# One transfer instead of two for each kept weight and sum, a new order of all steps, and the last stores in the order of their tiles

## The chip, the cores and the metric

The kernel runs on one core of one Trainium2 chip. The metric is the device time in microseconds of one execution. A core has a matrix engine (PE), a vector engine (DVE), a scalar engine (ACT), a general engine (POOL) and a queue engine that only issues transfers (SP). Each of them works through its own instructions strictly in order and waits for the others by semaphores. POOL issues transfers too.

## The reference

What is computed is linear attention, followed by a normalized and gated two-layer network. The shapes are 8 batches, 8 heads, 576 positions and 64 dimensions, so 4608 tokens of 512 numbers, and an inner width of 1536.

```
q_s = exp(q - max(q, axis=-1));  q_s = q_s / (sum(q_s, axis=-1) + 1e-9)
k_s = exp(k - max(k, axis=2));   k_s = k_s / (sum(k_s, axis=2) + 1e-9)
kv  = einsum('bhsd,bhse->bhde', k_s, v)
x   = einsum('bhsd,bhde->bhse', q_s, kv) -> 4608 x 512
xn  = x / sqrt(mean(x * x, axis=-1) + 1e-6) * rms_g
g   = xn @ w_gate;  val = xn @ w_val
out = (g * 1/(1 + exp(-g)) * val) @ w_out
```

The three weights come as 64-bit floats and are turned into 32-bit ones on the chip.

## The kernel before

**Precision.** Each matrix product is made in three passes: an operand is split into a high part that PE takes as it is and a low part (the rest), and high times high, high times low and low times high are added up in PSUM. Names that end in `_hi` and `_lo` are the steps that make these parts (a cast, then a subtraction).

**Tiling.** The 4608 tokens are nine blocks of 512. Blocks 0 to 2 are computed directly, in units s = 0 to 35: twelve units to a block, one for each 128 columns of the inner width. A unit has f1.s.0 and f1.s.1 (gate and value, 12 matmuls each, into the two banks of `ps_gv`), g_mul.s and h_mul.s (DVE, L965 and L972, which read and free those banks), silu.s (ACT), h_hi.s and h_lo.s, and f2.s (12 matmuls into the four banks of `ps_o`). Blocks 3 to 8 are three pairs in a scheme of Winograd: seven products (pp) on sums of weights and sums of inputs, DVE steps that combine them (c_...), then gate, hm, the split hp_hi and hp_lo, the second layer f2p and the stores put.p.t.n. The attention of a block runs in between, in small steps: k_load, k_max, k_diag, k_sub, k_exp, k_mm (the product of k and v, L566 on PE), kv_hi, kv_lo, and likewise q_load, q_max and so on. They use the two banks of `ps_a`. k and v tiles have two buffers each, q tiles three.

**Weights.** In block 0 the weights are loaded and converted (load_w, conv_...); in block 1 (units 12 to 23) they are split again and the split weights are kept: w_keep (L901), o_keep (L905) and, for sums of weights of the Winograd scheme, s_add, s_hi, s_lo and s_keep (L946) write them to DRAM from SP's queue. In the end of block 2 w_back and o_back, and in the pairs w_in and o_in, read them back by transfers that POOL issues.

**What sets the order.** A table of 3101 steps, the string ORDER, is written out by hand. The program goes through it from the front and calls each step's function; a letter behind a colon picks the engine (A is ACT, D is DVE, P is POOL), and without one the function's own is taken. So the table sets the order of each engine's instructions. Buffers, semaphores and the waits that follow from them are put in by the framework: a tile in a pool with n buffers waits until the tile n places ahead is read, and a transfer on SP is tied to one of eight semaphores, so that it also waits for the transfer eight ahead of it to land.

**The last steps.** put copies a finished bank of PSUM to SBUF and stores it (L1206). Of the tiles of the last group of tokens, number 2 and 3 are copied to tiles named `gs` and the rest to tiles named `ot`, which have two buffers; number 3 is copied and stored in two halves, by ACT (L1200) and DVE (L1202).

A helper `copy` records copies of several steps under one line (L388), and `scaled` under L395, k_diag's among them.

Of the kernel before, what the change touches and what calls it, by code (L numbers as in the profile page):

```python
# [27 lines left out]
load_w.1.1 k_load.1.0 q_eps0.0.0 q_eps0.0.2 k_tr.0.2 warm.2.2 q_rec0.0.0 k_max0.0.3 warm.2.10 load_w.0.2 q_rec0.0.2
q_mul0.0.0:P k_tr.0.3 k_top.0.2 load_w.2.0 q_max0.0.3 k_diag.0.2:A load_w.2.1 k_rows.0.2 q_mul0.0.2:P q_sum0.0.1
q_t0.0.0 q_load0.1.0 k_top.0.3 k_sub.0.2 q_sub0.0.3:P k_diag.0.3:A warm.2.11 q_c0.0.0:A k_rows.0.3 warm.2.3 k_eps.0.0  # L30
k_exp.0.2 load_w.1.2 k_sub.0.3 q_t0.0.2 load_w.3.0 q_exp.0.3 load_w.3.1 k_max0.0.1 k_mm.0.2 k_exp.0.3 load_w.2.2
load_w.3.2 q_eps0.0.1 k_rec.0.0 q_c0.0.2:A q_rec0.0.1 k_load.1.1 k_tr.0.1 q_sum0.0.3 warm.2.13 q_mul0.0.1:P
kv_norm0.0.0:A k_mm.0.3 k_top.0.1 k_eps.0.2 k_diag.0.1:A q_eps0.0.3 k_rec.0.2 conv_mul.0.0 q_load0.1.1 q_rec0.0.3
k_rows.0.1 k_eps.0.3 q_mul0.0.3:P q_x0.0.0 k_sub.0.1 kv_norm0.0.2:A conv_low.0.0.1 q_t0.0.1 k_rec.0.3 conv_shift.0.0
k_exp.0.1 q_load0.1.2 conv_sign.0.0 q_x0.0.2 x_hi.0.0:A conv_add.0.0.1 q_c0.0.1:A x_lo.0.0 warm.2.12 x_sq.0.2 warm.2.5
x_sq.0.0 k_mm.0.1 x_hi.0.2:A q_t0.0.3 conv_mul.0.1 k_eps.0.1 x_lo.0.2 kv_norm0.0.3:A v_ones.1.0 conv_shift.0.1 n_sum0.0
v_load.1.0 q_c0.0.3:A k_rec.0.1 conv_sign.0.1 conv_low.0.1.1 warm.2.6 q_x0.0.3 k_max.1.0 kv_norm0.0.1:A conv_add.0.1.1
# [5 lines left out]
w_hi.1.0.2:A f1.0.0.2.1 f1.0.0.2.2 f1.0.0.2.3 f1.0.1.2.0 conv_low.3.0.2 conv_sign.0.2 w_lo.1.0:P f1.0.1.2.1 f1.0.1.2.2
f1.0.1.2.3 n_rows.0 k_tr.1.0 conv_low.2.2.1 conv_add.0.2.1 k_top.1.0 g_mul.0 k_diag.1.0:A k_rows.1.0 q_sum0.1.0 f1.1.0
silu.0 w_lo.1.1:P load_w.4.0 k_sub.1.0 load_w.4.1 load_w.4.2 n_cols.0 v_ones.1.1 v_load.1.1 conv_mul.2.0 q_eps0.1.0
h_mul.0 conv_mul.2.1 conv_shift.2.0 f1.1.1 k_exp.1.0 conv_shift.2.1 conv_sign.2.0 conv_sign.2.1 conv_mul.1.2 q_rec0.1.0
f2.0 conv_add.2.0.2 g_mul.1 conv_mul.3.0 conv_shift.1.2 conv_low.3.2.1 conv_shift.3.0 silu.1 conv_sign.1.2 q_mul0.1.0:P
conv_sign.3.0 w_hi.2.0.2:A h_mul.1 conv_add.1.2.1 k_mm.1.0 q_load0.1.3 k_max.1.1 conv_mul.3.1 warm.2.9 w_lo.2.0:P
f1.2.0 conv_low.4.0.2 k_eps.1.0 load_w.5.0 conv_shift.3.1 load_w.5.1 w_lo.2.1:P conv_low.4.2.1 k_rec.1.0 load_w.5.2
conv_sign.3.1 k_load.1.2 kv_norm0.1.0:A q_max0.1.1 conv_add.3.0.2 conv_mul.2.2 q_t0.1.0 g_mul.2 kv_hi.1.0:A f1.2.1  # L50
q_c0.1.0:A conv_shift.2.2 silu.2 q_max0.1.2 conv_mul.4.0 conv_sign.2.2 q_sub0.1.1:P w_hi.3.0.2:A conv_shift.4.0
conv_add.2.2.1 q_x0.1.0 q_max0.1.3 q_exp.1.1 conv_sign.4.0 f2.1 w_lo.3.1:P load_w.6.0 x_hi.1.0:D load_w.6.1 x_sq.1.0
load_w.6.2 h_mul.2 q_sub0.1.2:P conv_mul.4.1 x_lo.1.0 conv_low.5.0.2 q_sub0.1.3:P conv_shift.4.1 q_sum0.1.1
conv_mul.3.2 v_ones.1.2 kv_lo.1.0:P f1.3.1 v_load.1.2 conv_sign.4.1 conv_low.5.2.1 w_lo.3.0:D conv_mul.4.2
conv_shift.3.2 conv_add.4.0.2 q_exp.1.2 conv_shift.4.2 q_exp.1.3 f1.3.0 conv_sign.3.2 conv_low.6.0.2 conv_sign.4.2
conv_add.3.2.1 conv_mul.5.0 k_max.1.2 w_hi.4.0.2:A conv_add.4.2.1 load_w.7.0 f2.2 conv_shift.5.0 conv_mul.5.1
load_w.7.1 g_mul.3 load_w.7.2 conv_low.6.2.1 w_lo.4.0:P load_w.8.0 conv_shift.5.1 silu.3 load_w.8.1 conv_sign.5.0
load_w.8.2 w_lo.4.1:P conv_sign.5.1 conv_mul.5.2 q_sum0.1.2 conv_add.5.0.2 k_tr.1.1 f1.4.0 o_hi.4:A k_top.1.1 h_mul.3
k_diag.1.1:A conv_shift.5.2 q_sum0.1.3 conv_low.7.0.2 o_lo.4:P conv_sign.5.2 k_rows.1.1 f1.4.1 k_sub.1.1 w_hi.5.0.2:A
conv_add.5.2.1 g_mul.4 k_exp.1.1 q_eps0.1.1 w_lo.5.0:P load_w.10.0 q_rec0.1.1 load_w.10.1 f2.3 load_w.10.2 q_mul0.1.1:D  # L60
conv_mul.6.0 w_lo.5.1:P conv_mul.6.1 q_load.2.0 conv_shift.6.0 silu.4 conv_shift.6.1 conv_sign.6.0 conv_sign.6.1
k_mm.1.1 o_hi.5:A h_mul.4 conv_add.6.0.2 conv_mul.7.0 f1.5.0 k_eps.1.1 h_hi.4:A k_rec.1.1 k_load.1.3 conv_shift.7.0
kv_norm0.1.1:A conv_sign.7.0 conv_low.8.0.2 h_lo.4:P q_t0.1.1 g_mul.5 w_hi.6.0.2:A f1.5.1 q_c0.1.1:D o_lo.5:P
conv_mul.7.1 conv_mul.6.2 conv_shift.7.1 w_lo.6.0:P silu.5 conv_shift.6.2 conv_low.7.2.1 conv_sign.7.1 w_lo.6.1:P f2.4
conv_low.8.2.1 conv_sign.6.2 conv_mul.7.2 conv_add.7.0.2 h_mul.5 conv_low.10.0.2 conv_shift.7.2 k_max.1.3 h_hi.5:A
q_x0.1.1 conv_low.10.2.1 conv_add.6.2.1 f1.6.0 conv_sign.7.2 x_hi.1.1:A q_max.2.0 x_sq.1.1 h_lo.5:P x_lo.1.1
w_hi.7.0.2:A q_half.2.0 conv_mul.8.0 conv_add.7.2.1 f1.6.1 g_mul.6 conv_mul.8.1 conv_shift.8.0 silu.6 w_lo.7.0:P
load_w.9.0 conv_shift.8.1 o_hi.6:A load_w.9.1 load_w.9.2 kv_hi.1.1:A conv_sign.8.0 x_acc.1.1:P f2.5 conv_sign.8.1
conv_mul.8.2 w_lo.7.1:P h_mul.6 conv_shift.8.2 h_hi.6:A conv_add.8.0.2 conv_sign.8.2 conv_mul.9.0 f1.7.0 o_hi.7:A
conv_shift.9.0 conv_sign.9.0 conv_mul.9.1 o_lo.6:P w_hi.8.0.2:A conv_shift.9.1 k_tr.1.2 f1.7.1 h_lo.6:P g_mul.7  # L70
conv_low.9.0.2 k_top.1.2 conv_sign.9.1 w_lo.8.0:P k_diag.1.2:A silu.7 conv_mul.9.2 q_eps0.1.2 v_ones.1.3 q_eps0.1.3
k_rows.1.2 q_rec0.1.2 conv_add.9.0.2 v_load.1.3 f2.6 h_mul.7 conv_low.9.2.1 k_sub.1.2 h_hi.7:A conv_shift.9.2 k_exp.1.2
q_rec0.1.3 conv_sign.9.2 q_mul0.1.2:P f1.8.0 o_lo.7:P q_load.2.1 w_hi.9.0.2:A w_lo.8.1:P q_t0.1.2 g_mul.8 w_lo.9.0:P
k_mm.1.2 q_c0.1.2:A silu.8 f1.8.1 k_eps.1.2 conv_add.9.2.1 k_load.2.0 k_rec.1.2 kv_norm0.1.2:D h_lo.7:P conv_mul.10.0
conv_mul.10.1 q_max.2.1 w_lo.9.1:P f2.7 kv_hi.1.2:A conv_shift.10.0 conv_shift.10.1 conv_add.8.2.1 conv_sign.10.0
conv_sign.10.1 q_mul0.1.3:P conv_mul.10.2 load_w.11.0 f1.9.0 load_w.11.1 h_mul.8 o_hi.8:A load_w.11.2 conv_add.10.0.2
conv_shift.10.2 o_hi.9:A q_load.2.2 h_hi.8:A k_max.2.0 q_x0.1.2 g_mul.9 o_lo.8:P w_hi.10.0.2:A conv_sign.10.2 f1.9.1
# [248 lines left out]
def linear_attention_then_gated_ffn(ctx: ExitStack, tc, q, k, v, w_gate, w_val, w_out, rms_g, out):  # L326
    nc = tc.nc
# [569 lines left out]
    def w_keep(s):  # L897
        i, odd = divmod(s % NF, 2)
        at = A21 if odd else A11
        for m in range(2):  # L900
            nc.sync.dma_start(wd[i][m][:, at:at + 2], wh_[s][:, m].bitcast(F32))  # L901
# [347 lines left out]
```

## Time and profile before

| | |
|---|---|
| median of 3 runs | 981.62 us (979.29 to 983.41) |
| the profiled execution | 976.97 us, its span 975.2 us |
| PE busy | 944.7 us, 97% of the span |
| DVE, ACT, POOL busy | 681.7, 456.5 and 524.7 us |
| mean granted clock of PE | 0.99 |
| transferred | 202.32 MB, mean 207 GB/s |
| kept weights and sums: transfers issued on SP | 24 of 512 KB (L901), 24 and 48 of 256 KB (L905, L946) |

The profile is of one execution. Its span runs from the first to the last instruction, and the time is a little longer. In timelines, a row has the start, the duration, the engine, the line of the kernel, the operation, what it writes and reads, and in brackets how long the engine had been idle and what released it. SPq is the queue of SP. A wait is put down to the one that came last.

### The profile page before, as it was taken

What the parts mean: (1) busy time and instruction counts of PE and PEld (TensorE: products, weight loads), DVE (VectorE), ACT (ScalarE), POOL (GpSimd) and SP (SyncE); (2) the same over time, 40 slices, a digit from 0 to 9 for tenths busy, and PEclk for the clock granted to TensorE, in tenths of its full rate; (3) what the DMA queues carried; (4) which work ended last, traced back from release to release, by engine and by line L of the source; (5) the groups of instructions that cost most, each with busy time, mean ns of one, the idle gap of its engine ahead of it and who ended that gap; (6) DMA issues with size and microseconds to landing.
All of it is one profiled execution on the core that took longest, in us unless ns stands there. A gap on an engine that the chain in (4) does not pass through costs nothing.

```text
span 975.2 us, 14167 instructions
## 1 busy us (share of the span) xinstructions
PE 944.7 (97%) x4681; PEld 760.8 (78%) x4681; DVE 681.7 (70%) x1436; ACT 456.5 (47%) x721; POOL 524.7 (54%) x557
## 2 busy tenths in 40 slices
...
GB/s 240 236 299 205 115 46 265 272 293 302 259 218 214 206 224 178 190 243 218 258 211 182 144 239 150 193 261 151 215 173 258 217 160 233 214 191 195 89 203 140
DMA packets 166836, 202.32 MB, mean 207 GB/s; under 512 B 105924, under 2 KB 127724, under 8 KB 162156
## 3 DMA queue, kind: packets, MB, share of 16 engines
...
HBM read 160.49 MB, written 40.89 MB: 207 GB/s over the span
## 4 chain that ended last, share of the span: by engine, by line
PE 75%; DMA 8%; DVE 7%; SPq 5%; issue 3%; ACT 1%; POOL 1%; DVEq 0%; ACTq 0%; POOLq 0%
PE ps_gv L1101 17%; PE ps_o L1101 12%; PE ps_gv L960 10%; PE ps_o L1188 10%; PE ps_a L1101 7%; PE ps_o L997 6%; PE ps_a L1188 5%; PE ps_gv L1188 5%; DMA qt<-in_q_dram 3%; SPq L634 2%; DMA kt<-in_k_dram 2%; PE ps_a L566 1%; DMA raw<-in_moe_w_val_dram 1%; SPq L946 1%; PE ps_a L772 1%
## 5 line engine op out<-in xcount | busy, mean ns | idle before, releaser
L960 PE MATMUL ps_gv<-xh,w 128*128 128x512 f32 x576 | 193.2, 402 | 0.2 <-DVE gs L972 0.2
L1101 PE MATMUL ps_gv<-x,ring 128*128 128x512 f32 x576 | 142.2, 392 | 0.0
L960 PEld LDWEIGHTS ps_gv<-xh,w 128*128 128x128 f32 x576 | 108.9, 189 | 26.0 <-issue 1.3
L1101 PEld LDWEIGHTS ps_gv<-x,ring 128*128 128x128 f32 x576 | 107.2, 188 | 22.5
L960 PE MATMUL ps_gv<-xl,w 128*128 128x512 f32 x288 | 112.7, 395 | 0.0
L1122 DVE TENSOR_TENSOR tmp<-tmp,ps_gv 128x512 f32<-128x512 f32 x84 | 57.3, 684 | 60.8 <-PE ps_gv L1101 57.3
L1074 POOL DMA_DIRECT2D ring<-wd x54 | 30.7, 568 | 127.6 <-PE ps_gv L1101 51.8
L1101 PE MATMUL ps_o<-x,ring 128*128 128x512 f32 x360 | 84.9, 389 | 0.0
L1101 PEld LDWEIGHTS ps_o<-x,ring 128*128 128x128 f32 x360 | 67.6, 188 | 14.1
L883 POOL TENSOR_TENSOR w<-w,w 128x512 fp32r<-128x512 f32 x42 | 56.0, 1346 | 20.4 <-ACT w L388 20.4
L997 PE MATMUL ps_o<-o,hh 128*128 128x512 f32 x256 | 66.2, 401 | 0.0
L388 ACT CAST hh<-gs 128x512 fp32r<-128x512 f32 x54 | 33.3, 617 | 68.2 <-DVE gs L1138 24.1
L960 PEld LDWEIGHTS ps_gv<-xl,w 128*128 128x128 f32 x288 | 54.7, 190 | 11.0 <-issue 0.6
L997 PEld LDWEIGHTS ps_o<-o,hh 128*128 128x128 f32 x256 | 47.6, 190 | 10.4 <-DVE o L891 0.2
L1122 DVE TENSOR_TENSOR tmp<-tmp,ps_o 128x512 f32<-128x512 f32 x42 | 28.6, 685 | 33.0 <-PE ps_o L1101 32.6
L1170 POOL TENSOR_TENSOR hl<-gs,hh 128x512 fp32r<-128x512 f32 x19 | 24.7, 1300 | 29.5 <-PE ps_gv L1101 14.5
L1101 PE MATMUL ps_a<-x,w 128*128 128x512 f32 x144 | 37.0, 392 | 3.1 <-issue 3.1
L519 DVE TENSOR_REDUCE cm<-kt 116x128 f32<-116x640 f32 x28 | 36.7, 1310 | 4.0 <-DMA kt<-in_k_dram 3.9
L388 ACT CAST w<-w 128x1024 fp32r<-128x1024 f32 x30 | 31.3, 1047 | 13.2 <-DMA wd<-w 7.3
L1188 PE MATMUL ps_o<-o,hh 128*128 128x512 f32 x144 | 37.4, 392 | 0.0
L1101 PE MATMUL ps_a<-x,ring 128*128 128x512 f32 x144 | 36.7, 390 | 0.6 <-DVE kt L554 0.6
L1101 PE MATMUL ps_gv<-x,w 128*128 128x512 f32 x144 | 36.8, 403 | 0.0
...
## 6 DMA issues: line engine op xcount, KB each, us to landing
...
```

What stands on the lines that cost most here:

```text
L388: (e.copy if e is nc.scalar else e.tensor_copy)(dst, src)
L519: nc.vector.tensor_reduce(out=cm, in_=kt_[b, g].rearrange("p h j d -> p h d j"), axis=AX.X, op=ALU.max)
L566: nc.tensor.matmul(pk[h * D:(h + 1) * D, :D + 1], lhsT=ke[:n, h, j], rhs=vt[:n, j, h], start=(j == 0), stop=(j == len(rows) - 1))
L634: nc.sync.dma_start(qt[p0:p0 + 32, c0 // 32:c1 // 32], q[b, 2 * g + h, s0:s0 + c1 - c0, 32 * f:32 * f + 32].rearrange("(m c) i -> c m i", ...
L883: on(nc.gpsimd).tensor_tensor(out=w[:, :, 1], in0=halves(s % NF, a, 1)[:, 0], in1=w[:, :, 0].bitcast(F32), op=ALU.subtract)
L960: nc.tensor.matmul(pd[s], lhsT=w[:, a, c // 2, m, c % 2 * P:c % 2 * P + P], rhs=X[j, c][x], start=(n == 1), stop=(n == 3 * NKT))
L997: nc.tensor.matmul(po[t], lhsT=a[:, t * P:(t + 1) * P], rhs=w, start=(i == 0 and n == 0), stop=(i == NF - 1 and n == len(terms) - 1))
L1074: nc.gpsimd.dma_start(t, src.rearrange("p a b f -> p (a b f)"))
L1101: nc.tensor.matmul(abc[p, i, m, b], lhsT=src[:, h, c * P:(c + 1) * P], rhs=operand(o, c, x), start=first and n == 0, stop=n == 5, skip_gro ...
L1122: nc.vector.tensor_tensor(out=dst, in0=ux[u + (src,)], in1=abc[u + (b,)], op=ALU.add)
L1170: on(nc.gpsimd).tensor_tensor(out=hl, in0=h_src(p, t, c), in1=HH[p, t, c][0].bitcast(F32), op=ALU.subtract)
L1188: nc.tensor.matmul(pa[p, t, k], lhsT=a[:, k * P:(k + 1) * P], rhs=w, start=(c == 0 and n == 0), stop=(c == NF - 1 and n == 2))
```

## The change

Three things change together.

First, w_keep, o_keep and s_keep each issue one transfer instead of two, for the high and the low part (w_keep, s_keep) or the two halves (o_keep) at once. For that the tile in DRAM that holds the weights of a group has both parts in one, and a helper `parts_of` picks the piece of it. w_back loads both parts in one transfer too.

```diff
-    wd = [[tc.dram_tile([P, 8, 2, HALF], F32, name=f"wd{i}_{m}") for m in range(2)] for i in range(NH)]
+    wd = [tc.dram_tile([2, P, 8, 2, HALF], F32, name=f"wd{i}") for i in range(NH)]
+    ot_ = {}
+
+    def parts_of(i, at, n):
+        return wd[i][:, :, at:at + n].rearrange("m p a b f -> p m a (b f)")
 
     def w_keep(s):
         i, odd = divmod(s % NF, 2)
-        at = A21 if odd else A11
-        for m in range(2):
-            nc.sync.dma_start(wd[i][m][:, at:at + 2], wh_[s][:, m].bitcast(F32))
+        nc.sync.dma_start(parts_of(i, A21 if odd else A11, 2),
+                          wh_[s].rearrange("p m a b f -> p m a (b f)").bitcast(F32))
 
     def o_keep(s):
-        for n in range(2):
-            nc.sync.dma_start(od[s % NF][:, n], wo_[s][n].bitcast(F32))
+        nc.sync.dma_start(od[s % NF], ot_[s].bitcast(F32))
 
     def w_back(s):
         i, odd = divmod(s % NF, 2)
-        at = A21 if odd else A11
-        w = w_tile(s)
-        for m in range(2):
-            nc.gpsimd.dma_start(w[:, m], wd[i][m][:, at:at + 2])
+        nc.gpsimd.dma_start(w_tile(s).rearrange("p m a b f -> p m a (b f)"), parts_of(i, A21 if odd else A11, 2))
...
     def s_keep(i, n):
-        for m in range(2):
-            nc.sync.dma_start(wd[i][m][:, {1: S1, 2: S2, 3: S3, 4: S4}[n]], split[i, n][:, m].bitcast(F32))
+        nc.sync.dma_start(parts_of(i, {1: S1, 2: S2, 3: S3, 4: S4}[n], 1)[:, :, 0],
+                          split[i, n].rearrange("p m b f -> p m (b f)").bitcast(F32))
...
-hp_lo.2.1.10:D f2p.2.1.10 hp_hi.2.1.11:A hp_lo.2.1.11:P f2p.2.1.11 put.2.1.0:D put.2.1.3:D put.2.1.1:D put.2.0.3:A
-put.2.0.1:A put.2.1.2:A
+f2p.2.1.10 hp_hi.2.1.11:D hp_lo.2.1.11:P f2p.2.1.11 put.2.1.0:A put.2.1.1:D put.2.1.2:A put.2.1.3:A put.2.0.1:A
```

Second, the table of steps is another one from its first line on. It has the same 3101 steps; 307 of them go to another engine than before (k_diag of four k tiles, 6.2, 6.3, 7.2 and 7.3, for example, from DVE to ACT). Third, its last steps, shown above, store the tiles of the last group in the order of their numbers; put.2.0.3 now stands further ahead, put.2.0.1 at the end.

Lines of the new kernel are two or three lower than those of the old one up to there (L901 is L902, L905 is L906, L946 is L943, L965 is L963, L972 is L970, L388 is L386).

In SP's queue, in unit 12, where the first weights and sums are kept (`wd` and `od` are the tiles in DRAM, `parts` a split sum), there stood:

```order
L901 DMA wd_0_118<-w 128x1024
L901 DMA wd_1_119<-w 128x1024
L901 DMA wd_0_118<-w 128x1024
L901 DMA wd_1_119<-w 128x1024
L1004 DMA out_dram<-ot 128x512 x2
L946 DMA wd_0_118<-parts 128x512
L946 DMA wd_1_119<-parts 128x512
L483 DMA kt<-in_k_dram 112x2x320
L483 DMA kt<-in_k_dram 3x2x320
L484 DMA kt<-in_k_dram 1x10x64
```

and now stands:

```order
L902 DMA wd_118<-w 128x2x1024 x2
L943 DMA wd_118<-parts 128x2x512
L1002 DMA out_dram<-ot 128x512 x2
L906 DMA od_124<-o 128x1024
L481 DMA kt<-in_k_dram 112x2x320
L481 DMA kt<-in_k_dram 3x2x320
L482 DMA kt<-in_k_dram 1x10x64
```

Four stores of two weights became two, two of a sum became one, and one store of W_out is now ahead of the load of the k tile.

On DVE, behind h_mul.11, the work up to g_mul.13 (the second row of `gs<-ps_gv,r` in each) was, from the point where the root mean square of block 1 is done:

```order
L849 STREAM_TRANSPOSE r<-y 128x512
L965 TENSOR_TENSOR gs<-ps_gv,r 128x512
L584 TENSOR_SCALAR rs<-ps_a 128x1
L554 TENSOR_TENSOR kt<-kt,ps_a 116x640
L700 TENSOR_REDUCE st<-qt 128x16
L588 RECIPROCAL rs<-rs 128x1
L965 TENSOR_TENSOR gs<-ps_gv,r 128x512
```

and now is, behind the row of the transpose (L847):

```order
L698 TENSOR_REDUCE st<-qt 128x16
L963 TENSOR_TENSOR gs<-ps_gv,r 128x512
L931 TENSOR_TENSOR sums<-w_92,sums 128x512
L711 TENSOR_REDUCE sw<-st 128x16
L890 TENSOR_TENSOR o<-w_92,o 128x512
L386 CAST parts<-sums 128x2x256
L940 TENSOR_TENSOR parts<-sums,parts 128x2x256
L759 TENSOR_TENSOR ql<-qT,qh 128x512
L940 TENSOR_TENSOR parts<-sums,parts 128x2x256
L582 TENSOR_SCALAR rs<-ps_a 128x1
L586 RECIPROCAL rs<-rs 128x1
L963 TENSOR_TENSOR gs<-ps_gv,r 128x512
```

A k_sub (`kt<-kt,ps_a`) went elsewhere; a step s_add (`sums`), a step o_lo (`o<-w,o`), a split of a sum (`parts`) and a further low part of one, and a q_lo came in. Ahead of these rows one more o_lo and a kv_lo came in as well.

At the end, ACT copied one half of tile 3, two `ot` tiles and a `gs` tile, in this order:

```order
L1200 COPY gs<-ps_a 128x256
L388 COPY ot<-ps_o 128x512 x2
L388 COPY gs<-ps_gv 128x512
```

and now copies tile 0 of the last group, tile 2, half of tile 3, and one `ot` tile of the group before:

```order
L386 COPY ot<-ps_a 128x512
L386 COPY gs<-ps_gv 128x512
L1198 COPY gs<-ps_a 128x256
L386 COPY ot<-ps_o 128x512
```

One of the two `ot` copies from `ps_o` moved ahead of these rows, and the other is the last.

More of the change, by code (lines that the diff above doesn't have):

```diff
@@ L28 @@
[L28 to L37, printed above, removed]
@@ L43 @@
[L43 to L52, printed above, removed]
@@ L53 @@
[L53 to L77, printed above, removed]
@@ L88 @@
-k_rows.2.0 kv_lo.1.3:P f1.12.1 n_y0.1 h_lo.11:P k_sub.2.0 w_keep.12 k_exp.2.0 s_add.0.1:D w_keep.13 n_y1.1 s_add.0.2:P
-k_tr.2.1 f2.11 s_hi.0.1:A s_add.0.3:P k_top.2.1 s_hi.0.2:A n_rows.1 k_diag.2.1:A s_lo.0.1:P g_mul.12 k_mm.2.0
-store.0.0:A s_lo.0.2:P store.0.1:A k_rows.2.1 k_eps.2.0 f1.13.0 k_sub.2.1 s_hi.0.3:A o_lo.12:P o_hi.13:A q_max.2.3
-s_keep.0.1 k_exp.2.1 k_rec.2.0 k_load.2.2 v_ones.2.3 kv_hi.2.0:A q_lo.2.0:P silu.12 k_mm.2.1 g_mul.13 s_keep.0.2
-s_lo.0.3:P q_half.2.3 f1.13.1 kv_lo.2.0 o_keep.12 w_hi.14.0.2:A o_lo.13:P q_max2.2.3 h_mul.12 s_keep.0.3 k_eps.2.1
@@ new lines @@
+q_hi.2.0:A q_lo.2.0:D s_lo.0.4:D q_sub.2.2:P f1.12.1 f2.11 store.0.2:A store.0.3:A silu.12 o_hi.13:A o_lo.13:P
+s_hi.0.2:A k_mm.2.0 k_eps.2.0 k_rec.2.0 kv_hi.2.0:A o_keep.12 k_load.2.2 s_keep.1.1 s_keep.0.4 v_ones.2.2 v_load.2.2
+s_add.0.3:P f1.13.0 w_hi.14.0.2:A g_mul.13 k_tr.2.1 k_top.2.1 h_mul.12 k_diag.2.1:A silu.13 h_hi.12:A o_keep.13
+store.0.0:A s_lo.0.2:D s_keep.0.2 store.0.1:D kv_lo.2.0 s_add.1.2:D h_lo.12:D s_add.1.4:P f1.13.1 k_rows.2.1 k_sub.2.1
+q_x.2.0 x_hi.2.0:A k_exp.2.1 x_lo.2.0 h_mul.13 h_hi.13:A x_sq.2.0 w_hi.15.0.2:A q_exp.2.2 s_hi.0.3:A q_sub.2.1:P
```

541 lines of the change are left out of this document (293 added, 248 removed).

## The prediction

> **What bounds the kernel now.** I read the busy time by stage first. Columns: stretch in us, its length, busy time of PE, PEld, DVE, ACT and POOL, granted clock, DMA share, GB/s.
>
> ```profile
> 0.00:100.00 100.00, 91.17 (x460) 62.81 (x461) 83.87 (x171) 81.12 (x128) 74.71 (x85) 0.98 0.87 245
> 150.00:225.00 75.00, 74.60 (x404) 60.67 (x402) 66.88 (x150) 51.44 (x80) 44.61 (x41) 1.00 0.87 298
> 225.00:400.00 175.00, 165.96 (x935) 133.34 (x935) 151.75 (x382) 118.52 (x190) 136.16 (x133) 0.98 0.83 224
> 525.00:600.00 75.00, 70.80 (x343) 57.20 (x342) 67.91 (x126) 37.16 (x61) 36.69 (x42) 0.98 0.55 168
> 600.00:950.00 350.00, 350.00 (x1545) 289.76 (x1544) 168.98 (x277) 60.74 (x104) 112.19 (x138) 1.00 0.62 198
> 950.00:976.00 26.00, 17.18 (x76) 13.89 (x74) 4.88 (x9) 3.27 (x6) 5.50 (x6) 0.88 0.42 139
> ```
>
> PE sets the pace: from 600 to 950 it is busy for 350.00 of 350 us. The change issues the same matmuls in nearly the same order, so nothing is to be had there. What an order of steps can change is PE's idle time: 8.8 us before 100, 0.4 in 150 to 225, 9.0 in 225 to 400, 4.2 in 525 to 600 and 8.8 at the end (differences of the first two figures of each row). Next, the list of what PE waited for in 225 to 400: total, times, longest.
>
> ```profile
> PE ps_a L566 <- ACT kt L558: 3.9, 4, 2.3
> PE ps_a L566 <- ACT sq L789: 2.2, 1, 2.2
> ```
>
> 6.1 of the 9.0 us are waits of L566, the k-times-v products of the attention part (k_mm). They cost more than their length, as a finer cut of the stretches shows:
>
> ```profile
> 250.00:275.00 25.00, 23.81 (x123) 18.93 (x122) 20.99 (x56) 17.49 (x31) 19.52 (x17) 0.94 0.79 248
> 350.00:375.00 25.00, 22.67 (x111) 18.18 (x110) 18.66 (x58) 12.44 (x20) 20.07 (x22) 0.93 0.92 226
> 525.00:550.00 25.00, 21.89 (x108) 17.42 (x107) 20.50 (x43) 12.88 (x20) 14.29 (x16) 0.93 0.72 222
> ```
>
> The granted clock falls to 0.94, 0.93 and 0.93 in just the stretches with the longest waits. A mean lower by 0.06 or 0.07 over 25 us is 1.5 to 1.75 us of matmul work lost on top of each wait; I take 1.7. The Trainium skill ("TensorE: Matmul & The Clock Gate", Part 1: The HAM clock gate) puts the fall to half clock behind an idle window of about 3.4 us. The waits here are 2.2 to 3.1 us long, so the trace is stricter than that figure; by the page alone no wait below would cost more than its length, and the sum would be 2.5 us nearer to nothing.
>
> **Term 1, the stall at 545.** It is the longest single wait. Timeline rows of DVE, POOL and PE, then the group of L395 on DVE (minimum/median/maximum in ns):
>
> ```profile
> 539.76 4.19 DVE L395 TENSOR_SCALAR cm<-ident,kx 128x128 f32<-128x128 f32 x1
> ...
> 540.12 1.30 POOL L1020 TENSOR_TENSOR xl<-xl,r 128x512 f32<-128x512 f32 x1
> 541.38 1.27 POOL L1158 TENSOR_TENSOR w<-w,tmp 128x512 f32<-128x512 f32 x1
> 542.61 1.25 POOL L1170 TENSOR_TENSOR hl<-xh,hh 128x512 fp32r<-128x512 f32 x1
> ...
> 545.14 1.83 PE L1101 MATMUL ps_a<-x,w 128*128 128x512 f32 x6 [3.11 <-issue]
> ...
> L395 DVE TENSOR_SCALAR cm<-ident,kx x4: 275/330/4192, 458.7 to 539.8; 128x128 f32<-128x128 f32 x4
> ```
>
> A 128x128 scaling (k_diag) that has a median of 330 ns took 4192 ns, and ended when POOL's run of three tensor operations did, at 543.9. Behind it on DVE stood the two kv_lo operations (L608), which free the bank that PE's next product needs; PE stood still for 3.11 us. The Trainium skill ("SBUF — State Buffer", Who interferes with whom) says why such a thing can be: the two engines share a pair of ports under an exclusive lock. The change gives all four of these scalings to ACT, and puts kv_lo ahead of the DVE work that it stood behind, with about 2.8 us of matmuls between it and the product concerned (six of them take 1.83 us in the row of PE above). ACT is busy for 37.16 of 75 us there, which covers one more scaling of 0.3 us. So the wait and its clock loss go: 3.1 + 1.7 = **4.8 us less**. Bounds: all of it, or 1.6 if half the wait and the clock loss come back as a wait for the next step in that bank.
>
> **Term 2, attention between 225 and 400.** How the first long wait came about is in the chain of waits (start, us, what):
>
> ```profile
> 232.86 0.69 SPq L946
> ...
> 237.59 1.20 SPq L946
> 238.84 0.68 SPq L634
> ...
> 242.84 2.03 DMA qt<-in_q_dram
> ...
> 247.89 0.87 PE ps_a L566 x19
> ...
> 301.59 8.37 DMA kt<-in_k_dram
> ```
>
> From 232.9 to 238.8 the chain runs through SP's queue, which was issuing the kept weights and sums (L946, L905, L901) ahead of the q loads (L634) that the attention steps wait for. What those issues cost stands in the groups of the three lines (minimum/median/maximum in ns, first and last start):
>
> ```profile
> L901 SPq DMA_DIRECT2D wd<-w x24: 344/488/1183, 152.3 to 254.3; - x24
> L905 SPq DMA_DIRECT2D od<-o x24: 367/434/1205, 162.7 to 271.9; - x24
> L946 SPq DMA_DIRECT2D wd<-parts x48: 334/444/1200, 158.6 to 297.0; - x48
> ```
>
> 96 issues become 48. At the medians that removes 12 x 0.488 + 12 x 0.434 + 24 x 0.444 = 21.7 us of SP's time between 152 and 297, if a merged issue costs what a single one did. The rows speak for that: a 512 KB transfer (L901) takes 488 ns to issue and a 256 KB one (L905, L946) 434 and 444, so a doubled size adds about a tenth. The other end is nothing: a merged issue that costs two. The bytes are the same. Every q, k and v load behind those stores is issued earlier, and the new order also puts the steps between a k load and its k_mm elsewhere. In their favour at the most: 9.0 us of waits and two clock losses of 1.7, together 12.4. Against it speaks the last row above: 8.37 us of the chain at 301 are the transfer of a k tile itself, at a DMA share of 0.83 over the stretch, and no issue that is saved shortens that; and DVE is busy for 151.75 of 175 us here, so it can become the next to be late. I take **half, 6 us less**. Bounds: 12.4 less, to 4 more (two new waits of some 2 us, the size of the two long rows).
>
> Twelve loads of POOL (w_back) become six; POOL is busy for 136.16 of 175 us and PE's list has no long wait for it, so I put nothing down for that. Stored data are read back much later than they are written, so a later landing of a merged store costs nothing.
>
> **Term 3, DVE in unit 12.** Here the new order takes cover away. f1.13.1 needs the bank that g_mul.13 (L965) frees. The DVE timeline, and then the groups in 150 to 225 with the mean ns of one:
>
> ```profile
> 158.35 0.82 DVE L554 TENSOR_TENSOR kt<-kt,ps_a 116x640 f32<-116x640 f32 x1 [0.24 <-PE ps_a L548]
> 161.09 0.69 DVE L965 TENSOR_TENSOR gs<-ps_gv,r 128x512 f32<-128x512 f32 x1 [1.25 <-PE ps_gv L960]
> ...
> L883 DVE TENSOR_TENSOR w<-w,w 128x512 fp32r<-128x512 f32 x10 | 8.9, 902 | 1.4 <-ACT w L388 1.4
> L933 DVE TENSOR_TENSOR sums<-w 128x512 f32<-128x512 f32 x8 | 5.4, 681 | 0.0
> L942 DVE TENSOR_TENSOR parts<-sums,parts 128x512 fp32r<-128x512 f32 x6 | 4.1, 683 | 0.0
> L891 DVE TENSOR_TENSOR o<-w,o 128x512 fp32r<-128x512 f32 x3 | 2.0, 678 | 0.0
> L761 DVE TENSOR_TENSOR ql<-qT,qh 128x512 fp32r<-128x512 f32 x2 | 1.4, 682 | 0.0
> ```
>
> Before, DVE waited 0.24 + 1.25 = 1.5 us for PE on the way to g_mul.13: that is its slack. Between h_mul.11 and g_mul.13 the new order adds on DVE one s_add (L933, 0.68), two s_lo (L942, 1.37), two o_lo (L891, 1.36), one q_lo (0.68), a cast and a kv_lo (about 0.4 and 0.3, estimated from 128x512 operations of 0.68 as the smaller ones they are), and takes out one k_sub (L554, 0.82) and a small one: 4.8 - 0.9 = 3.9 us. 3.9 - 1.5 = 2.4 us of wait, as long as the ones that cost a clock loss before. I take the wait and half of the loss: **3.3 us more**. Bounds: nothing, if DVE arrives ahead, since an earlier part of its queue is lighter; and 7 if in addition POOL slows those ten operations, as it does the ten of L883 (902 against some 680 ns, 0.22 each, 2.2 us), with the whole loss.
>
> **Term 4, the tail.** The timeline of the last 11 us:
>
> ```profile
> 965.18 0.69 DVE L388 COPY ot<-ps_a 128x512 f32<-128x512 f32 x1 [4.96 <-PE ps_a L1188]
> ...
> 966.79 0.39 PE L1188 MATMUL ps_a<-o,hl 128*128 128x512 f32 x1
> 967.21 0.37 ACT L1200 COPY gs<-ps_a 128x256 f32<-128x256 f32 x1 [5.59 <-PE ps_a L1188]
> ...
> 968.00 0.58 ACT L388 COPY ot<-ps_o 128x512 f32<-128x512 f32 x1 [0.41 <-DMA out_dram<-ot]
> ...
> 968.67 3.12 SPq L1206 DMA_DIRECT2D out_dram<-ot  x3
> 970.84 0.58 ACT L388 COPY ot<-ps_o 128x512 f32<-128x512 f32 x1 [2.25 <-DMA out_dram<-ot]
> ...
> 971.94 0.33 SPq L1206 DMA_DIRECT2D out_dram<-gs  x1
> ```
>
> The last matmul ends at 967.2, the last store is issued at 971.94. Tiles named ot have two buffers: the copy at 968.00 waits until the store of the tile copied at 965.18 has landed, the one at 970.84 until that of the tile copied next, issued at 968.67, has. In the new order three ot copies are left in this row, the first as soon as its sum is done (965.2) and only the last one waits, for the landing that in this trace let the copy at 968.00 go. That copy ends at 968.6, its store follows: 971.9 - 968.6 = **3.3 us less**. Other end: it waits for the second store instead, issued at about 967.3, and lands 2.2 later: 969.5 + 0.6 = 970.1, 1.8 less.
>
> **The start** is in another order too: the first weights land later and the rest earlier, and DVE has as much work before unit 7 as it had. PE idles for 8.8 us there; I take 0, bounds 3 less to 3 more (a third of that idle time each way).
>
> Sum: -4.8 - 6 + 3.3 - 3.3 = -10.8 us. Against the profiled execution's 976.97 that is 966.2; this execution lies 4.65 below the median, so for the median 981.62 - 10.8 = **970.8, predicted 971**. Differences within 0.5% (4.9 us) are what a measurement of this kernel can't tell from no change.
>
> **The rivals.**
> 1. *Forecast*, as summed: 971, chance 0.49.
> 2. *SP's issue time was covered.* The loads are bound by their transfers (8.37 us for one k tile, DMA share 0.83), or merged issues cost double, and the attention waits come back elsewhere: term 2 is 0, the rest stays, -4.8 + 3.3 - 3.3 = -4.8: 976.8, on the edge of no change. Against it: 5.9 us of the chain before the wait at 247.9 are SP's alone. 0.24.
> 3. *All waits go*: -4.8 - 12.4 - 3.3 and no wait in unit 12, -20.5: 961. For it: every one of these waits is single and short. Against: DVE at 87% of the stretch. 0.12.
> 4. *DVE becomes the bound in 150 to 400.* It is busy for 66.88 + 151.75 = 218.6 of 250 us, and the new order has it prepare weights and sums earlier. If each of units 12 to 17 behaves like unit 12 in term 3, six waits of 2.4 with four clock losses are 14.4 + 6.8 = 21.2 more; with -4.8 - 3.3 that is +13: 995. It decides from three such waits on (+12.3, so +4 with the two sure terms). Against: the listed work of DVE rises by only some 6 us over the whole kernel, mostly moved, not added. 0.15.
>
> Faster: case 1, case 3 and a few of case 2 (0.02) make 0.63; no change 0.23; slower 0.14, since case 4 with two or three waits ends within the bound. The likeliest case by itself spans 964 to 978; the range takes in most of cases 2 and 3 and the milder end of case 4: **962 to 986**.
>
> **What would show it.** Term 1: no DVE row of 4 us at 540, no PE wait of 3 us before 600, and no clock below 0.98 in 525 to 550. Term 2: PE's wait list for 225 to 400 at about half of 9 us, 48 store issues of about 0.5 us each on SP; if they take 0.9, case 2. Term 3: one wait of 2 to 3 us of L958 for DVE's g_mul near 160; more of the kind make case 4. Term 4: the last store issued 1.4 to 1.8 us behind the last matmul instead of 4.7. The prediction is wrong if PE's idle time before 600 does not shrink by at least 5 us, or if it grows in the first 100.

## The result, and the profile after

| | before | changed kernel |
|---|---|---|
| median of 20 runs | 980.82 us (978.15 to 986.03) | 976.15 us (972.2 to 982.02) |
| ratio | | 0.9948, 95% interval 0.9932 to 0.9964 |
| the profiled execution | 976.97 us | 977.94 us |

The change takes 0.52% off, about 5.1 us. Forecast were 10.8 us, so the sign was right and the size half. Single executions of one kernel lie up to 6 us from its median, and the two profiled ones happen to lie on opposite sides: by them alone the changed kernel would be 1 us slower. Whatever follows on microseconds of a stage is therefore read, where it can be, from waits and rows that come back in several profiles, and gains are taken from the ratios of medians.

Busy time by stage, after (columns as in the prediction):

```profile
150.00:225.00 75.00, 69.68 (x388) 55.82 (x387) 70.79 (x153) 54.54 (x87) 52.85 (x46) 0.98 0.83 278
225.00:400.00 175.00, 169.23 (x927) 137.52 (x926) 160.35 (x366) 115.46 (x181) 133.63 (x123) 0.98 0.78 223
400.00:525.00 125.00, 122.37 (x653) 99.50 (x652) 105.95 (x270) 66.74 (x102) 79.75 (x87) 1.00 0.84 220
525.00:600.00 75.00, 71.99 (x367) 58.71 (x366) 60.56 (x126) 30.81 (x54) 36.81 (x43) 0.98 0.68 205
950.00:976.00 26.00, 21.55 (x96) 17.50 (x94) 6.37 (x11) 4.00 (x7) 5.22 (x7) 1.00 0.56 181
```

PE's idle time went from 0.4 to 5.3 us in 150 to 225, from 9.0 to 5.8 in 225 to 400, from nothing to 2.6 in 400 to 525, and from 4.2 to 3.0 in 525 to 600. Over all stretches before 600 it rose from 22.5 to 25.8. DVE is busy for 160.35 of 175 us in the second stretch (151.75 before). Over the whole span it is busy for 700.8 us against 681.7, and instructions that were added explain less than half of these 19 us (an estimate of some 8 us, from the counts of each form and the shorter of its two mean times). What PE waited for after, from the lists for 150 to 225, 225 to 400 and 400 to 600:

```profile
PE ps_a L546 <- ACT cm L391: 2.4, 1, 2.4
...
PE ps_a L1099 <- DVE kt L552: 3.3, 1, 3.3
PE ps_a L564 <- ACT sq L787: 0.6, 1, 0.6
...
PE ps_o L820 <- DVE ql L806: 3.0, 1, 3.0
```

The k-times-v products (now L564) wait for 0.6 us instead of 6.1: the loads behind them are no longer late. But two new waits of 3 us for DVE stand in the list, and one of 2.4 for a scaling on ACT that in turn waits for DVE. Their clock losses, again in stretches of 25 us:

```profile
150.00:175.00 25.00, 21.50 (x121) 16.63 (x120) 22.84 (x50) 17.65 (x28) 15.16 (x14) 0.93 0.76 269
375.00:400.00 25.00, 21.71 (x105) 17.47 (x104) 23.81 (x41) 11.16 (x18) 16.91 (x17) 0.86 0.61 163
575.00:600.00 25.00, 21.99 (x92) 17.73 (x91) 20.45 (x44) 10.80 (x18) 12.63 (x15) 0.93 0.67 196
```

And what DVE and POOL did ahead of the wait at 387, and DVE ahead of the one at 590, from the timelines:

```profile
379.31 6.38 DVE L1055 TENSOR_TENSOR x<-xl,x 128x512 fp32r<-128x512 f32 x1
...
379.56 1.30 POOL L1055 TENSOR_TENSOR x<-xh,x 128x512 fp32r<-128x512 f32 x1
380.79 0.57 POOL L1072 DMA_DIRECT2D w<-wd  x1
381.38 1.30 POOL L1055 TENSOR_TENSOR x<-xh,x 128x512 fp32r<-128x512 f32 x1
382.63 1.29 POOL L1055 TENSOR_TENSOR x<-ot,x 128x512 fp32r<-128x512 f32 x1
383.88 1.25 POOL L1055 TENSOR_TENSOR x<-xl,x 128x512 fp32r<-128x512 f32 x1
...
585.38 5.20 DVE L806 TENSOR_TENSOR ql<-acc,qh 128x512 fp32r<-128x512 f32 x1
```

It is the picture of the stall at 545 once more, at other places. A subtraction (step b_lo.0.4.1) that takes 0.69 us when nothing stands in its way took 6.38, and ended 0.6 us behind POOL's run of work (385.1, DVE at 385.7). n_lo.7 took 5.20. Both read two tiles in SBUF, and both are among the steps that the new order puts elsewhere: n_lo.7 was on POOL, and b_lo.0.4.1, on DVE already, now meets four POOL steps in a row, with one issue of a transfer between them.

### The profile page after: what moved, and what is told of

It reads as the page before. It is cut to its first block, busy times and chain, and to the rows that moved or that the text cites. A ratio compares the mean times of both kernels' runs of the same rounds, so it can differ in the third digit from the quotient of the medians.

```text
span 976.2 us, 14097 instructions
## 1 busy us (share of the span) xinstructions
PE 945.7 (97%) x4681; PEld 761.4 (78%) x4681; DVE 700.8 (72%) x1447; ACT 443.0 (45%) x704; POOL 526.5 (54%) x551
## 4 chain that ended last, share of the span: by engine, by line
PE 80%; DVE 9%; DMA 4%; SPq 2%; ACT 2%; issue 1%; ACTq 0%; DVEq 0%
PE ps_gv L1099 16%; PE ps_gv L958 15%; PE ps_o L1099 12%; PE ps_o L1186 10%; PE ps_o L995 7%; PE ps_a L1099 6%; PE ps_a L1186 5%; PE ps_gv L1186 5%; PE ps_a L564 2%; PE ps_a L770 1%; DMA kt<-in_k_dram 1%; DVE x L1055 1%; DMA qt<-in_q_dram 1%; DMA wd<-w 1%; DVE w L882 1%
## 5 line engine op out<-in xcount | busy, mean ns | idle before, releaser
L1099 PE MATMUL ps_gv<-x,ring 128*128 128x512 f32 x576 | 144.5, 396 | 1.4 <-DVE tmp L1120 1.4
L386 ACT CAST hh<-gs 128x512 fp32r<-128x512 f32 x50 | 30.9, 618 | 93.7 <-DVE gs L1136 50.8
L882 POOL TENSOR_TENSOR w<-w,w 128x512 fp32r<-128x512 f32 x44 | 60.2, 1377 | 13.6 <-ACT w L386 11.7
L1084 POOL DMA_DIRECT2D o<-od x36 | 19.8, 550 | 40.5 <-PE ps_a L1186 20.9
L1072 POOL DMA_DIRECT2D w<-wd x18 | 10.0, 558 | 46.3 <-PE ps_a L1099 27.0
```

Of the source, the lines that this page charges most:

```text
L386: (e.copy if e is nc.scalar else e.tensor_copy)(dst, src)
L882: on(nc.gpsimd).tensor_tensor(out=w[:, :, 1], in0=halves(s % NF, a, 1)[:, 0], in1=w[:, :, 0].bitcast(F32), op=ALU.subtract)
L1072: nc.gpsimd.dma_start(t, src.rearrange("p a b f -> p (a b f)"))
L1084: nc.gpsimd.dma_start(WO[n % 4], od[c])
L1099: nc.tensor.matmul(abc[p, i, m, b], lhsT=src[:, h, c * P:(c + 1) * P], rhs=operand(o, c, x), start=first and n == 0, stop=n == 5, skip_gro ...
```

## The experiments

All ratios are against the kernel before, run beside it on the same chip.

### One part at a time

**The last stores alone.** In the table of before, only the end is changed:

```diff
+put.2.0.3:D hp_hi.2.1.5:A
...
-put.2.1.0:D put.2.1.3:D put.2.1.1:D put.2.0.3:A put.2.0.1:A put.2.1.2:A
+put.2.1.0:A put.2.1.1:D put.2.1.2:A put.2.1.3:A put.2.0.1:A
```

> The kernel before with nothing but its last stores in the order of their tiles (put.2.0.3 goes ahead of the last group, too). Theory: the end of the kernel is set by a chain of copies that wait for landings of stores, so 3.0 to 3.4 us go (ratio 0.9966) and the last store is issued 1.4 to 1.8 us behind the last matmul. Rival: the landing of the last store sets the end whatever its order, so less than 1.5 us go.

Measured: 0.9972 (0.9955 to 0.9988), 2.7 us less. The end of its timeline:

```profile
972.80 0.39 PE L1187 MATMUL ps_a<-o,hl 128*128 128x512 f32 x1
...
973.90 0.58 ACT L387 COPY ot<-ps_o 128x512 f32<-128x512 f32 x1 [0.30 <-DMA out_dram<-ot]
...
974.58 0.40 SPq L1205 DMA_DIRECT2D out_dram<-ot  x1
```

The last store is issued 1.4 us behind the end of the last matmul (973.2), where it was 4.8. That is 3.4 us by the rows and 2.7 by the medians, with 3.4 well within the interval. The theory holds.

**The merged transfers alone.** The functions of the changed kernel with the table of before:

```diff
-        for m in range(2):
-            nc.sync.dma_start(wd[i][m][:, at:at + 2], wh_[s][:, m].bitcast(F32))
+        nc.sync.dma_start(parts_of(i, A21 if odd else A11, 2),
+                          wh_[s].rearrange("p m a b f -> p m a (b f)").bitcast(F32))
```

> The order of steps of before, with one transfer instead of two in w_keep, o_keep, s_keep and w_back. Theory of term 2: SP's issue time delays the q and k loads, so 3 to 6 us go and the waits of the k-times-v products between 225 and 400 shrink from 6.1 us to 3 or less; 48 store issues take about 0.45 to 0.5 us each. Rival: the loads are bound by their transfers, or merged issues cost double (0.9 us); the time is within 1.5 us of before.

Measured: 0.9908 (0.9892 to 0.9924), 9.0 us less, more than the 3 to 6 expected and more than the whole change brings. Its groups of store issues (minimum/median/maximum in ns):

```profile
L904 SPq DMA_DIRECT2D wd<-w x12: 360/404/1218, 155.1 to 251.5; - x12
L908 SPq DMA_DIRECT2D od<-o x12: 330/406/1153, 165.6 to 269.7; - x12
L945 SPq DMA_DIRECT2D wd<-parts x24: 364/420/1790, 162.0 to 294.9; - x24
```

The k-times-v products in PE's wait list for 225 to 400:

```profile
PE ps_a L566 <- ACT kt L558: 2.3, 4, 0.9
```

And that stretch as a whole, with two of 25 us:

```profile
225.00:400.00 175.00, 167.80 (x964) 135.42 (x963) 156.33 (x394) 120.12 (x193) 135.45 (x127) 1.00 0.84 229
250.00:275.00 25.00, 22.73 (x126) 18.20 (x126) 22.14 (x56) 17.52 (x31) 19.04 (x17) 1.00 0.80 249
350.00:375.00 25.00, 24.17 (x124) 19.48 (x123) 20.90 (x61) 12.91 (x22) 21.19 (x22) 1.00 0.95 223
```

A merged issue costs no more than a single one did (404 to 420 ns against 434 to 488). The waits of the k-times-v products fall from 6.1 us to 2.3, none is longer than 0.9, and the clock stays at 1.00 in both stretches where it had fallen. That is 3.8 us of these waits and some 3.3 of clock. But other short waits took part of their place: PE's idle time in the whole stretch went only from 9.0 to 7.2 us. And the profiled execution, at 974.76 us, is the slowest of its six and only 2.2 us ahead of the one of before. So the profile shows which waits went, but not how the whole 9.0 us of the medians come about.

How much late loads cost differs between profiles: in that of the tail experiment, which has the old transfers, one such product waited 4.1 us for the load of a v tile. Whether merging also makes the single times more alike isn't shown. They lie between 971.3 and 974.8 here (six runs), but as close together with the new order and split transfers (976.5 to 978.2), and further apart with merged transfers and two more edits (962.9 to 970.6).

**The order alone.** The new table, last stores included, in the code of before (two transfers each):

```diff
-ORDER = (table of before)
+ORDER = (table of the changed kernel)
```

> The order of steps of the changed kernel (last stores included) with two transfers for each kept weight and sum, as before. If merging carries what the change gains beside the tail, this is 2 to 5 us slower than the changed kernel (977 to 981). If merging is worth nothing, it is the changed kernel's 976 within 1.5 us, and beside the tail's 3.3 the new order is worth 1 to 2 us.

Measured: 0.9951 (0.9936 to 0.9965), 4.8 us less: the changed kernel's 0.9948 without its merged transfers. From its wait lists:

```profile
PE ps_a L564 <- ACT sq L787: 0.9, 1, 0.9
PE ps_a L564 <- DVE sw L711: 0.4, 1, 0.4
...
PE ps_a L1099 <- DVE kt L552: 3.3, 1, 3.3
...
PE ps_o L820 <- DVE ql L806: 3.0, 1, 3.0
```

With split transfers, too, the k-times-v products hardly wait in the new order, and the two waits for DVE are there with the same lengths. So in the new order merging gains nothing more. This fits merging and the new order removing the *same* late loads, a gain that can be had once.

**k_diag on ACT alone.** In the table of before:

```diff
-k_diag.6.2:D  k_diag.6.3:D  k_diag.7.2:D  k_diag.7.3:D
+k_diag.6.2:A  k_diag.6.3:A  k_diag.7.2:A  k_diag.7.3:A
```

> The order of before with k_diag of the four k tiles 6.2, 6.3, 7.2 and 7.3 on ACT instead of DVE, nothing else. Theory of term 1: the scaling on DVE is held by POOL's run of operations, so PE's 3.1 us wait at 545 and the low clock behind it go, and the time falls by 3 to 4.8 us. Rival 1: DVE is held at whichever of its operations comes there next, and the wait moves by one step: within 1.5 us of before, and the profile shows another DVE row of over 2 us between 535 and 600. Rival 2: the hold is in few executions, so the median does not move though the profile shows no wait.

Measured: 0.9948 (0.9930 to 0.9967), 5.1 us less, as much as the whole change. Its clock around the former stall:

```profile
525.00:550.00 25.00, 25.00 (x145) 20.12 (x144) 20.55 (x52) 15.57 (x23) 16.93 (x20) 1.00 0.72 209
```

PE is busy for all of it, at full clock. In every profile of a kernel that has k_diag.7.3 on DVE at this place (before, last stores alone, merged transfers alone, and two more below) the scaling took 4.2 us, so this hold does not depend on chance. Rival 1, a hold that moves on by one step, is out here: 3.1 us of waiting are gone from 525 to 600 and only the two short waits of before are left.

**The three gains together,** in the table of before: merged transfers, last stores, k_diag.

> The order of before with the three edits that gained alone: merged transfers (-9.0 us measured), last stores in order (-2.7), the four k_diag on ACT (-5.1). If they act at separate places, they add to -16.8: about 965 (ratio 0.983). If two of them gain from the same slack, it is 968 to 972. If a new wait takes their place as in the new order, it is 973 or more.

Measured: 0.9832 (0.9804 to 0.9860), 965.7 us; and once more later, 0.9829 (0.9794 to 0.9865). The three add up (expected 965). This kernel is 1.2% faster than the changed one, so what the change lost was lost by the rest of its new order.

### What the rest of the new order costs

**The two held steps to POOL.** In the changed kernel:

```diff
-b_lo.0.4.1:D
+b_lo.0.4.1:P
...
-hm.0.5.12:P ... n_lo.7:D
+n_lo.7:P hm.0.5.12:P ...
```

> The changed kernel with the two DVE operations that were held there for 6.4 and 5.2 us given to POOL (b_lo.0.4.1, and n_lo.7 one place further ahead). Theory: an operation of DVE with two inputs in SBUF is held while POOL runs its own without a gap; with the two gone, PE's waits of 3.3 us at 387 and 3.0 us at 590 and their clock losses go, so 5 to 9 us less than the changed kernel: 967 to 971. Rival: POOL gets 1.3 us more to do for each at its fullest places, and what waits for POOL is as late as it was: 974 to 978.

Measured: 0.9926 (0.9906 to 0.9946) where the changed kernel has 0.9948: 2 us, not clear of noise, less than the low end of what the theory expected (5 us) and within the rival's range. The waits of 3.3 and 3.0 us did go, but in its list for 400 to 600 stand two that are new or twice as long:

```profile
PE ps_a L770 <- DVE kv_lo L606: 3.5, 1, 3.5
PE ps_gv L1099 <- DVE tmp L1120: 2.9, 1, 2.9
```

and other steps b_lo on DVE took 5.47, 4.77 and 3.36 us there. The hold went to the next operations that read two tiles in SBUF.

**The four POOL steps beside the hold to DVE,** which gives DVE more to do:

```diff
-b_lo.0.1.0:P  b_lo.0.1.1:P  b_lo.0.2.0:P  b_lo.0.4.0:P
+b_lo.0.1.0:D  b_lo.0.1.1:D  b_lo.0.2.0:D  b_lo.0.4.0:D
```

> The changed kernel with the four operations beside the held one (b_lo.0.1.0, 0.1.1, 0.2.0 and 0.4.0) moved from POOL to DVE, which so has more to do. Theory of the hold: with POOL idle, b_lo.0.4.1 takes its 0.69 us, the five together 3.5 us where the one alone took 6.4, and PE's 3.3 us wait at 387 goes or falls below 1.5 us; n_lo.7, left as it is, stays held: 3 to 5 us less than the changed kernel (971 to 973). If DVE were simply late for its amount of work, the four more would make it later by 2.8 us: PE's wait at 387 is 6 us, the time 979.

Measured: 0.9937 (0.9916 to 0.9958), not to be told from the changed kernel and outside both expectations. But its DVE timeline decides between the two readings:

```profile
378.56 0.68 DVE L1055 TENSOR_TENSOR x<-xh,x 128x512 fp32r<-128x512 f32 x1
379.85 0.69 DVE L1055 TENSOR_TENSOR x<-xh,x 128x512 fp32r<-128x512 f32 x1 [0.61 <-ACT x L386]
380.46 0.68 DVE L1055 TENSOR_TENSOR x<-ot,x 128x512 fp32r<-128x512 f32 x1
381.07 1.29 DVE L1055 TENSOR_TENSOR x<-xl,x 128x512 fp32r<-128x512 f32 x2
382.38 0.69 DVE L963 TENSOR_TENSOR gs<-ps_gv,r 128x512 f32<-128x512 f32 x1
...
389.85 4.83 DVE L1055 TENSOR_TENSOR x<-xh,x 128x512 fp32r<-128x512 f32 x1
```

With POOL idle from 379 to 387.7, all five take their 0.65 to 0.69 us, 3.3 us together, where one alone took 6.38 before: DVE with four operations more is done earlier (382.4 instead of 385.7), and PE's wait there falls from 3.3 to 0.7 us. That DVE was late at this place for its amount of work is refuted. Its next operation beside a busy POOL, at 389.9, is held for 4.83; DVE has no gap behind it, and at 398.8 PE has waited 3.3 us for its kv_lo. n_lo.7, untouched, again took 5.20.

**Unit 12 relieved.** Six steps around it from DVE to POOL, in the changed kernel:

```diff
-o_lo.11:D  o_lo.12:D  s_add.0.1:D  s_lo.0.4:D  s_lo.1.1:D  q_lo.2.0:D
+o_lo.11:P  o_lo.12:P  s_add.0.1:P  s_lo.0.4:P  s_lo.1.1:P  q_lo.2.0:P
```

> The changed kernel with six operations of unit 11 to 13 given from DVE to POOL, which has gaps there (o_lo.11, o_lo.12, s_add.0.1, s_lo.0.4, s_lo.1.1, q_lo.2.0: 4.1 us of DVE). Theory of term 3: DVE's overload makes PE wait 2.4 us for k_diag at 153 and 0.9 us for g_mul.13 at 165 in the changed kernel, with a clock of 0.93 in 150 to 175; with the six gone both waits fall below 0.5 us, unit 14 starts 4 to 5 us earlier, and 3 to 5 us of it remain in the time (971 to 973). Rival: the waits go, but DVE's holds at 387 and 590 set the pace behind it and the time stays within 1.5 us of the changed kernel's 976.

Measured: 0.9956 (0.9938 to 0.9975). Nothing gained, and the wait, 2.4 us in the changed kernel, didn't go either:

```profile
147.04 1.38 DVE L600 TENSOR_TENSOR kv_lo<-ot,kv_hi 128x128 fp32r<-128x128 f32 x1
148.35 4.04 DVE L882 TENSOR_TENSOR w<-w,w 128x512 fp32r<-128x512 f32 x3
152.31 0.27 DVE L537 TENSOR_REDUCE kx<-ps_a 128x1 f32<-128x116 f32 x1
...
148.36 1.81 POOL L931 TENSOR_TENSOR sums<-sums,w 128x512 f32<-128x512 f32 x1
150.13 1.70 POOL L931 TENSOR_TENSOR sums<-w 128x512 f32<-128x512 f32 x1
...
153.06 0.48 PE L546 MATMUL ps_a<-cm,ones 128*116 128x128 f32 x2 [3.39 <-ACT cm L391]
```

Two of the six stood ahead of the reduction that k_diag waits for. Without them DVE starts it at 152.31, in the changed kernel with them at 152.21. The four operations left took 5.4 us beside POOL's; in the changed kernel the same four took 3.3, with kv_lo at 0.28 us and one w_lo at 0.69. Work that goes from DVE to POOL here comes back as time for which DVE is held.

**One more hold in the best kernel.** In the first profile of the three gains together, DVE took 5.14 us for h_lo.24 and PE waited for it:

```profile
279.57 5.14 DVE L980 TENSOR_TENSOR hl<-gs,hh 128x512 fp32r<-128x512 f32 x1
...
284.77 1.78 PE L996 MATMUL ps_o<-o,hl 128*128 128x512 f32 x4 [3.22 <-DVE hl L980]
```

```diff
-h_lo.24:D
+h_lo.24:P
```

> The kernel with the three gaining edits (merged transfers, last stores in order, four k_diag on ACT), and one operation more given from DVE to POOL: h_lo.24, which DVE took 5.14 us for at 279.6 while POOL ran four operations without a gap, so that PE waited 3.22 us in f2.24. Theory of the hold: on POOL it takes 1.3 us behind one operation, the wait falls below 0.5 us, and 3 to 5 us go against the kernel without this edit: 961 to 963. Rival: the next operation of DVE with two inputs in SBUF (q_mul.3.3) is held in its place; within 1.5 us.

> The kernel with the three gaining edits again, on the same chip as the one with h_lo.24 moved, so that the two are compared side by side: 964 to 967.

Measured: 0.9831 (0.9802 to 0.9860) with the edit and 0.9829 (0.9794 to 0.9865) without: no difference. In the second profile of the same unedited kernel that hold wasn't there; the longest DVE row from 270 to 300 was 1.78 us. So this one comes and goes between executions, unlike those of k_diag.7.3 (4.2 us in every profile that has it on DVE) and n_lo.7 (5.20 in each of the four that have it on DVE). A hold seen in a single profile isn't yet a cause of the median.

### What about the transfers gains

**As many issues as before, with the data merged.** Behind each merged store SP issues one more transfer, of 512 bytes:

```diff
+    def extra():
+        n = len(issued)
+        issued.append(n)
+        nc.sync.dma_start(scr[n:n + 1], ones[0:1, :])
...
         nc.sync.dma_start(od[s % NF], ot_[s].bitcast(F32))
+        extra()
```

> The order of before with the merged transfers, and behind each merged store of a kept weight or sum one more transfer of 512 bytes to an unused place, so that SP issues as many transfers as before while the data go in the merged ones. The unused transfers are the only addition. If it is SP's issues (their time, and the tie of each to the one eight ahead) that delay the loads, most of the 9.0 us comes back: 978 to 982. If the larger transfers themselves are what is better, it stays at 973 to 975.

Measured: 0.9953 (0.9933 to 0.9972), 4.6 us below before where the merged kernel is 9.0 below. About half of the gain is lost with 48 tiny transfers more, so their number on SP counts, with the data merged. But one profile doesn't bear out that it is all by late loads. In it the k-times-v products wait for 3.6 us, between the 2.3 of the merged kernel and the 6.1 of before, and a further wait of 3.3 us comes from h_lo.24, held on DVE for 5.17 us, the hold that came and went in the best kernel.

**As many transfers as before, half of them issued by ACT:**

```diff
-            nc.sync.dma_start(wd[i][m][:, at:at + 2], wh_[s][:, m].bitcast(F32))
+            (nc.sync, nc.scalar)[m].dma_start(wd[i][m][:, at:at + 2], wh_[s][:, m].bitcast(F32))
```

> The kernel before with two transfers for each kept weight and sum, the second one of each issued by ACT instead of SP: SP issues as few as with merged transfers, and the transfers are as small and as many as before. If SP's issues are the whole cause of the merged kernel's 9.0 us, this is 973 to 975, plus what 48 issues on ACT cost (ACT is not the bound there: 0 to 3 us). If the number of transfers is a part of it, as the 4.9 of 9.0 us that came back with extra issues on SP leave room for, it is 976 to 979.

Measured: 0.9997 (0.9974 to 1.0019): no gain at all, outside both expectations. SP issues as few stores as in the merged kernel, 12, 12 and 24. But its list of what SP waited for, from 150 to 310, has landings of other transfers in it:

```profile
SPq L946 <- DMA kt<-in_k_dram: 3.9, 3, 1.9
SPq L508 <- DMA wd<-parts: 3.0, 1, 3.0
SPq L483 <- DMA wd<-parts: 2.2, 1, 2.2
```

A load of v (L508) and one of k (L483) wait for stores to land. All its waits for landings add up to 17.7 us; in the same list of before there is one, of 2.4 us. That would fit a tie to the transfer eight ahead that counts transfers whoever issues them, which no run shows by itself. How the 9.0 us divide between the time of SP's issues and that tie is not settled: ACT also got 48 issues to do. And this profile has a loss that before doesn't have, PE idle for 3.6 us ahead of the product at 437.7 with a clock of 0.86 from 425 to 450, long after the last kept store (295.9). Whether it recurs isn't known, so a gain that is lost there isn't excluded either.

## Why the prediction was right in sign and half right in size

**Term 4, the tail (3.3 less): right.** The last stores alone gave 2.7 us by the medians, and in the changed kernel, too, the last store is issued 1.4 us behind the end of the last matmul (at 972.94 and 971.56).

**Term 1, the stall at 545 (4.8 less): right,** in place, cause and size. k_diag alone gave 5.1 us, the wait of 3.1 and its clock loss together. But in the changed kernel the stretch keeps little of it, as another hold comes in at 590.

**Term 2, the late loads (6 less, a half of what there was): mechanism right, sized too small, and given to the wrong part.** Merging alone took 9.0 us off. The prediction doubted it because transfers are long (8.37 us for a k tile); yet the runs point to when they began. But in the changed kernel merging adds nothing (0.9948 with, 0.9951 without), where the late loads have hardly any waits left without it. The sum counted the two as one term, which hid that they may be two ways to the same gain.

**Term 3, DVE in unit 12 (3.3 more): right in sign and stretch, too small, and mostly at another step.** Forecast was a wait of 2 to 3 us for g_mul.13; that one was 0.7. The longest is 2.4 us for k_diag, ahead of it. With smaller ones, PE's idle time from 150 to 225 rose by 4.9 us, at a clock of 0.93 from 150 to 175. The cause is open in part. Ahead of the wait for k_diag, two w_lo on DVE were held for about 1.1 us (two others take 1.29 together at 171.77 in the same profile):

```profile
149.93 2.36 DVE L882 TENSOR_TENSOR w<-w,w 128x512 fp32r<-128x512 f32 x2
```

The rest of DVE's time there is listed work, as the term has it. But taking six of these operations away gained nothing, since POOL then held those that were left, which the prediction had only in its bound.

**The step that failed** is that the sum lets new waits for DVE come at one place, unit 12, and takes holds of DVE as a term that only goes away. The stages show it, with those of the kernel with the three gains (its second profile) beside the rows of before and after above:

```profile
150.00:225.00 75.00, 74.95 (x404) 61.13 (x403) 68.39 (x150) 52.74 (x82) 46.01 (x43) 1.00 0.90 301
225.00:400.00 175.00, 167.19 (x959) 134.54 (x959) 156.70 (x393) 119.71 (x193) 133.31 (x126) 1.00 0.84 228
400.00:525.00 125.00, 125.00 (x669) 102.57 (x668) 99.77 (x247) 68.15 (x103) 66.71 (x75) 1.00 0.82 218
525.00:600.00 75.00, 73.92 (x363) 60.21 (x362) 67.52 (x136) 40.05 (x64) 42.43 (x45) 1.00 0.61 191
```

The table has PE's idle time plus the clock's loss in us, in one profile of each kernel. The loss is one less the granted clock, times the length; since the clock is given to 0.01, it is uncertain by up to 0.9 us.

| stretch | before | changed | three gains | changed less before | forecast |
|---|---|---|---|---|---|
| 150 to 225 | 0.4 + 0 | 5.3 + 1.5 | 0.1 + 0 | +6.4 | +3.3 (term 3) |
| 225 to 400 | 9.0 + 3.5 | 5.8 + 3.5 | 7.8 + 0 | -3.3 | -6 (term 2) |
| 400 to 525 | 0 + 0 | 2.6 + 0 | 0 + 0 | +2.6 | nothing |
| 525 to 600 | 4.2 + 1.5 | 3.0 + 1.5 | 1.1 + 0 | -1.2 | -4.8 (term 1) |

Forecast were 7.5 us less here, and these profiles have 4.5 more. Two of the signs that the prediction names went against it: PE's idle time before 600 did not shrink by 5 us but grew by 3.3, and PE waits of 3 us stand before 600. Since the profiled execution of before lies 3.9 us below its median and the changed kernel's 1.8 above, the table shows where time went, and not how much of the medians each stretch makes. The loss in 150 to 225 is no chance of one profile: PE is idle there for 5.0 to 6.1 us in all five profiles of the new order, and for 0.6 or less in all others.

The prediction saw the mechanism at 540, found k_diag taken off DVE, and didn't look for operations with two inputs in SBUF that the new order newly puts beside a run of POOL work. Two that matter in the later stretches are b_lo.0.4.1 (6.38 us) and n_lo.7 (5.20). PE waits for 3.3 + 3.0 = 6.3 us on them, and in this profile the clock loses (0.14 + 0.07) x 25 = 5.25 us around them. But the longest loss against the kernel with the three gains is the one around unit 12, with 6.8 us. There the rows of DVE show only shorter holds, of 1 to some 2 us.

By the medians, -2.7 (tail) - 5.1 (k_diag) - 9.0 (loads in time, once) = -16.8, which the kernel with the three gains shows to be there. The changed kernel has -5.1, so the rest of its new order costs 11.7 us. How they divide between holds, listed work of DVE and the clock is not shown: with the holds at 387 and 590 gone together, only some 2 us came back by the medians, as other holds took their place. That DVE would become the bound was rival 4, which had the engine right; its price was reckoned from the amount of listed work, unit for unit, and at least the waits at 387 and 590 came from the company of that work.

The Trainium skill ("SBUF — State Buffer", Who interferes with whom) says that an operation of DVE with two inputs in SBUF contends with one of POOL that reads SBUF, and that one blocks for the whole of the other's instruction. The traces agree, and go beyond: DVE's operation wasn't let in after one POOL operation of 1.3 us but was done only behind a run of four, after 6.38 us. One thing the rows leave open: DVE's operation starts at 379.31, ahead of the first of POOL's four at 379.56, and is held all the same.
